# Row tiles of two GLU layers turned by DMA instead of TensorE, with 41 DMA issues moved to ScalarE's queue

## The chip, the core and the metric

The kernel runs on one core of a Trainium2 chip, in one launch. The metric is the device time of the launch in microseconds; a time without more is the median of several runs. A profiled execution, taken by the hardware profiler, has its own time, and a span: from the first recorded instruction to the last.

The engines are named as the profile names them: PE (TensorE: matmuls, and transposes, which are matmuls with the identity), PEld (its weight loads), DVE (VectorE), ACT (ScalarE), POOL (GpSimd) and SP (SyncE, which here only issues DMAs). Each runs its own instructions in order and waits on semaphores for the others. The letter q behind a name (SPq, ACTq) marks the engine's queue instructions, DMA issues among them.

## The reference: what is computed

Four residual blocks on a sequence of 2048 rows of 512 in bf16, forward, and then all gradients for a given `grad_out`. Blocks 0 and 2 are linear attention with 32 heads of 16, blocks 1 and 3 a gated linear unit (GLU) with F = 1376. Blocks 0 and 2 share their weights, and so do 1 and 3. Cut to what matters:

```python
def A(h):                                  # h = layernorm(x), no scale or shift
    q, k, v = heads(h @ wqkv)
    pq, pk = phi(q), phi(k)                # t + 1 for t > 0, else exp(t); + 1e-6
    kv, z = pk^T v, sum(pk)                # per head, over the whole sequence
    o = (pq @ kv) / (pq . z + 1e-6)
    return o @ wo

def B(h):
    g, u = h @ w_gate, h @ w_up
    return (sigmoid(g) * u) @ w_down

x = x + A(layernorm(x)); x = x + B(layernorm(x))
x = x + A(layernorm(x)); x = x + B(layernorm(x))
# returned: x, and the gradients by A_x, A_wqkv, A_wo, B_w_gate, B_w_up, B_w_down
```

## The kernel before, in words

**Layers and row tiles.** Layers are numbered 0 to 3 (0 and 2 attention, 1 and 3 GLU). The rows are cut into 16 tiles (`st`) of 128, which are handled in 8 pairs. The residual `k.xs[st]` stays on the chip. For the backward pass the forward pass stores to HBM the normalized rows (`sv_h`), of the attention the rows pq divided by their denominator (`sv_pqn`), and of the GLU the sigmoid with its derivative product (`sv_ssd`) and the gated product in 32x32 block-transposed form (`sv_hdd`, `sv_hdl`).

**The stages the change touches.** `ab_fwd` (L1058) runs twice: at L202 for layer 1, at L233 for layer 3. It does the tail of the attention layer before it (the products of turned pq rows with `kv` and `wo`, added to the residual) and the whole GLU layer. After a prelude for tiles 0 to 3 come rounds i = 1 to 7, one for each further pair, with `st = 2i` the first tile of the pair whose gate and up products are computed.

**A round.** It holds six units `gu` (L1090 and on; `CUNITS`, L1054). A unit takes two chunks of 128 columns of F for the 256 rows of the pair: eight matmuls of 256 columns into a `g` bank of PSUM, eight into a `u` bank. Unit 5 has a single chunk, so half of that. Then:

- L1106 and L1107 (ACT): sigmoid of g into `ssd_t`, sigmoid of -g into `oms`;
- L1108 (DVE): `hhT` = u times the sigmoid, which reads the `u` bank;
- L1109 (POOL): the derivative product into the second half of `ssd_t`;
- L1112 (SP): the store of `ssd_t` to `sv_ssd`.

Between the units stand, in the order written at L1186 to L1225:

- `A.attn_y` for the two tiles of the next pair (`attn_y` ends in an add on DVE to the residual, followed by the statistics of their LayerNorm);
- `A.pair_front1` and `pair_front2` (L962): for the pair two further on, DVE divides pq by its denominator (`den`, L969 and on); two DMA transposes on SP (L977) turn `pqnstage` (128x512 each) into `pqnT`; L979 stores the rows;
- `after` (L1131): in layer 1 the LayerNorm apply of the next layer, in layer 3 the rounding of the final rows into a staging tile and its store, one for each pair (`out_cb`, L221; the store is L229);
- `down_mm`: 11 matmuls of 512 columns with `w_down` for a tile of an earlier pair, and the add to the residual on DVE;
- `ln.apply(st + 2)` before unit 3 and `ln.apply(st + 3)` behind it (`FwdLN.apply`, L546): ACT writes the normalized rows (L529) into `hstage`, a pair to a buffer; the second call also issues the store to `sv_h` (L556);
- `trs`: block transposes of `hhT` on DVE (L1047, 768 columns at a time), each stored from SP (L1050, to `sv_hdd`/`sv_hdl`);
- `ln.stage_T` (L558) near the round's end: eight PE transposes (L569) of the pair's `hstage` into a bank of PSUM, and one evacuation on ACT (L380) into `hT`. `hT` is what all matmuls of the next round's units read (L1090). The rounds with a next pair, i = 1 to 6, have one;
- `fills`: turns of weight pieces for the backward pass, in small portions, and `turn_weights`: the DMAs of `fill` one by one, each ordered behind the `sv_ssd` store of the last unit. In layer 1 these are DMA transposes of weights with their stores (L429, L430), in layer 3 also 12 plain loads of turned weight pieces (L466, L468).

The units' order in rounds 1 to 6 is 0, 1, 2, 3, 5, `stage_T`, 4; in round 7, where `stage_T` does nothing, 4 and 5 follow each other (L1215, L1218).

**What sets the order.** On PE, ACT, DVE and POOL the instructions stand in the program's order. SP's order is chosen by a scheduler, so a DMA of SP need not stand where the program has it. A DMA issued from ACT (`nc.scalar.dma_start`) stands in ACT's program order, between the computing instructions. All DMAs of both queues share eight semaphores, in turn, so each waits for the one eight before it.

**Buffers.** PSUM: bank `t` x2, `g` x2, `u` x2, `y` x1, `ln` x1. SBUF: `hstage` 2 (the staging tile of the final rows in layer 3 takes turns with it), `hT` 2, `oms` 2, `ssd_t` 5 in layer 1; in layer 3 three, and two more named `ssd_q`; `pqnstage` 2, `pqnT2` 2.

Of the kernel before, what the change touches and what calls it, by code (L numbers as in the profile page):

```python
# [9 lines left out]
BF16 = mybir.dt.bfloat16  # L10
# [12 lines left out]
P = 128  # L23
NST = S // P
NDC = D // P
NFC = (F + P - 1) // P
# [39 lines left out]
def kernel(  # L66
# [18 lines left out]
    nc = tc.nc  # L85
# [3 lines left out]
    k = K()  # L89
# [4 lines left out]
    out0 = out_0.rearrange("b s d -> (b s) d")  # L94
# [52 lines left out]
    with tc.tile_pool(name="wfwd", bufs=1, reuse_waits="tile") as wfwd, ExitStack() as lctx, tc.manual_schedule(engines=EM):  # L147
# [27 lines left out]
        def load_wd():  # L175
# [16 lines left out]
            hT=lctx.enter_context(tc.tile_pool(name="ln_hT", bufs=2, reuse_waits="tile")),  # L192
# [3 lines left out]
        with tc.tile_pool(name="aq0", bufs=1, reuse_waits="tile") as aq:  # L196
            A = kq_fwd(k, aq, 0, lns[0], lns[1], x_bf)
# [5 lines left out]
        with tc.tile_pool(name="aq2", bufs=1, reuse_waits="tile") as aq:  # L203
            ocur, bw = {}, {}
            k.g_in = g_in
            k.g_from_input = 3
            k.sv[3]["gbf"] = g_in

            def open_bwd():
                xctx.close()  # L210
                bw["wb"] = bctx.enter_context(tc.tile_pool(name="wbwd", bufs=1, side="right", reuse_waits="tile"))
                prectx = ExitStack()
                k.pre = dict(pool=prectx.enter_context(tc.tile_pool(name="pre", bufs=1, side="right",
                                                                    reuse_waits="tile")), close=prectx.close)
                bw["B3"] = BBwd(k, 3)

            A = kq_fwd(k, aq, 2, lns[2], lns[3])
            open_bwd()
            wb, B3 = bw["wb"], bw["B3"]

            def out_cb(st):  # L221
                if st % 2 == 0:
                    ocur["t"] = k.lnres["stg"].tile([P, 2, D], BF16, name="out0_t", tag="hstage")
                if st >= NST - 2:
                    nc.gpsimd.tensor_scalar(ocur["t"][:, st % 2, :], k.xs[st][:], 1.0, 0.0, ALU.mult, ALU.add)
                else:
                    nc.scalar.copy(ocur["t"][:, st % 2, :], k.xs[st][:])
                if st % 2 == 1:
                    nc.sync.dma_start(out=dram_batch(out0, st // 2, 2), in_=ocur["t"][:])  # L229

            fill = Fill(wT_groups_b(k, wb), wT_dmas_b(k))
            A.tail(fill)
            ab_fwd(k, A, lns[3], fill, out_cb=out_cb, bwd=B3)  # L233

    if True:
# [80 lines left out]
        last = 2 * D // GW * NDC  # L316
# [6 lines left out]
        T = {}  # L323
# [61 lines left out]
def batch_rows(b, nb=NB):  # L385
    return slice(b * nb * P, (b + 1) * nb * P)


def dram_batch(ap2d, b, nb=NB):
    return ap2d[batch_rows(b, nb), :].rearrange("(n p) d -> p n d", p=P)  # L390
# [64 lines left out]
def wT_dmas_b(k):  # L455
    nc = k.nc
    view = lambda d: d.rearrange("(c p) f -> p c f", p=P)
    parts, h = [], F // 2
    for r0, r1, c0 in ((0, h, 0), (h, F, WDT)):
        parts.append((k.wdT[:, WDT:NDC, r0:r1], k.w_in["wd"][r0:r1, WDT * P:D],  # L460
                      [(view(k.wT["wdT"][c0 * P:(c0 + 2) * P, :]), k.wdT[:, c0:c0 + 2, :])]))
    jobs = wT_dmas(k, parts)
    for nm, t in (("wu", k.wuT), ("wg", k.wgT)):
        for c in range(0, NFC - 1, 2):
            e = c + 2
            jobs.append(lambda nm=nm, t=t, c=c, e=e: nc.sync.dma_start(out=t[:, c:e, :],  # L466
                                                                       in_=view(k.wT[nm + "T"][c * P:e * P, :])))
        jobs.append(lambda nm=nm, t=t: nc.sync.dma_start(out=view(k.wT[nm + "T"][(NFC - 1) * P:, :]),  # L468
                                                         in_=t[:, NFC - 1:, :]))
    return jobs  # L470

# [53 lines left out]
def ln_apply(k, x_t, h_out, nmr, rstd, quick=False):  # L525
    if quick:
        k.nc.vector.tensor_scalar(h_out, x_t, nmr, rstd, ALU.subtract, ALU.mult)
        return
    k.nc.scalar.activation(h_out, x_t, ACT.Identity, bias=nmr[:], scale=rstd)  # L529


class FwdLN:
# [10 lines left out]
        if st < NST:  # L543
            self.nmr[st] = ln_stats(self.k, self.k.xs[st][:], self.rstd(st), st < 1)

    def apply(self, st):  # L546
        if st >= NST:
            return
        k, nc, l = self.k, self.k.nc, self.l
        if st % 2 == 0:  # L550
            self.cur = k.lnres["stg"].tile([P, 2, D], BF16, name="hstage", tag="hstage")
        h_t = self.cur[:, st % 2, :]
        self.hs[st] = h_t
        ln_apply(k, k.xs[st][:], h_t, self.nmr.pop(st), self.rstd(st), st < 1)
        if st % 2 == 1:
            nc.sync.dma_start(out=dram_batch(k.sv[l]["h"], st // 2, 2), in_=self.cur[:])  # L556

    def stage_T(self, sts, evac="scalar", bank="ln"):  # L558
        if sts[0] >= NST:
# [341 lines left out]
def attn_fronts(k, A, pool, small):  # L901
    nc = k.nc
    sva = k.sv[A.l]
    cur, F_ = {}, {}
# [57 lines left out]
    def pair_front2(i, turned=True):  # L962
        if i >= NST // 2:
            return
        f = F_[2 * i]
        den = f["den"]
        pqn = pool.tile([P, 2, D], BF16, name="pqnstage", bufs=2)
        rden = A.rden_all[:, 2 * i:2 * i + 2, :].rearrange("p n h -> p (n h)")
        nc.vector.tensor_scalar(den[:], den[:], EPS, None, ALU.add)  # L969
        nc.vector.reciprocal(rden, den[:])  # L970
        nc.vector.tensor_tensor(pqn[:].rearrange("p n (h e) -> p (n h) e", h=H),
                                A.pq_pairs[i][:].rearrange("p n (h e) -> p (n h) e", h=H),
                                rden.unsqueeze(2).to_broadcast([P, 2 * H, DH]), ALU.mult)
        if turned:
            pqnT = pool.tile([P, 2, NDC, P], BF16, name="pqnT2", bufs=2)
            for j in range(2):
                nc.sync.dma_start_transpose(out=pqnT[:, j, :, :], in_=pqn[:, j, :])  # L977
                F_[2 * i + j] = dict(T=pqnT[:, j, :, :])
        nc.sync.dma_start(out=dram_batch(sva["pqn"], i, 2), in_=pqn[:])  # L979
        f["pqn"] = pqn  # L980

    def pair_front3(i):
        if i >= NST // 2:
# [9 lines left out]
            F_[2 * i + j] = dict(T=pqnT[:, j, :, :])  # L993

    A.pair_prod, A.pair_front1, A.pair_front2, A.pair_front3 = pair_prod, pair_front1, pair_front2, pair_front3

    def attn_mm(st, bank="y"):
        if st >= NST:
            return
        pqnT = F_[st]["T"]  # L1000
        y_ps = F_[st]["y"] = ps_tile(k, bank, [P, D], F32, "y_ps")
        for c in range(NDC):
            nc.tensor.matmul(y_ps[:], lhsT=pqnT[:, c, :], rhs=A.M_sb[:, c, :],
                             start=(c == 0), stop=(c == NDC - 1))
# [49 lines left out]
CUNITS = [(c, min(2, NFC - c)) for c in range(0, NFC, 2)]  # L1054
# [3 lines left out]
def ab_fwd(k, A, ln, fill, nxt=None, out_cb=None, bwd=None):  # L1058
    nc, tc = k.nc, k.tc
    la, l = A.l, A.l + 1  # L1060
    sva, sv = k.sv[la], k.sv[l]
    with ExitStack() as ctx:
# [114 lines left out]
        for i in range(1, NPAIR):  # L1177
            st = 2 * i
            last = i == NPAIR - 1
            nf = fill.share(i, NPAIR - 1)  # L1180

            def trs(n):
                for _ in range(min(n, len(pend))):
                    trans(*pend.pop(0))
            nt = 1 if i < NPAIR - 2 else 2
            gu(st, 2, *CUNITS[0])  # L1186
            if l == 3 and i > 1:
                turn_weights()
            A.attn_y(st + 2, "t")
            A.attn_y(st + 3, "t")  # L1190
            A.pair_front1(i + 2)
            after(st - 3)
            gu(st, 2, *CUNITS[1])
            A.pair_front2(i + 2)
            trs(nt)
            fills((nf + 2) // 3)
            gu(st, 2, *CUNITS[2])
            if l == 3 or i % 2 == 0:
                turn_weights()
            if i > 1:  # L1200
                down_mm(st - 2)
            ln.apply(st + 2)
            if last:
                trans(NBLK - 1, 0)
            gu(st, 2, *CUNITS[3])
            if l == 3:
                turn_weights()
            down_mm(st - 1, "t")
            ln.apply(st + 3)
            A.pair_prod(i + 3)  # L1210
            fills(nf // 3)
            trs(nt)
            if last:
                trans(NBLK - 1, 1)
            gu(st, 2, *CUNITS[4 if last else 5])  # L1215
            ln.stage_T([st + 2, st + 3], bank="t")
            after(st - 2)
            gu(st, 2, *CUNITS[5 if last else 4])  # L1218
            if l == 3:
                turn_weights()  # L1220
            fills((nf + 1) // 3, "vector")
            if l == 1 and last:
                nc.scalar.activation(k.tab[:], k.neg[:], ACT.Exp)
            if i % 2 == 1 and not last:
                pend += [(i // 2, g) for g in range(NG + 1)]  # L1225
            if i == NPAIR - 3 and bwd is not None:
                bwd.load_g(0)
# [920 lines left out]
```

## Time and profile before

| | |
|---|---|
| time, median of 3 runs | 1109.11 us (1108.24 to 1110.34) |
| the profiled execution's own time | 1108.52 us |
| its span | 1106.8 us |
| mean clock granted to TensorE | 0.998 of full speed |
| moved by DMA | 268.25 MB, mean 242 GB/s |
| PE transposes of `stage_T` (L569) | 128, from 69.2 to 374.3 us |
| evacuations into `hT` on ACT (L380) | 16, 1.01 us each for a pair |
| DMA transposes on SP (L977) | 20, median issue 1.26 us, from 98.2 to 354.4 us |
| stores `sv_h<-hstage` from SP | 16 of 256 KB, median 3.8 us from issue to landing |
| stores `sv_pqn<-pqnstage` from SP | 16 of 256 KB, median 2.4 us from issue to landing |

How to read it: times are microseconds from the span's start. The share of an engine is its busy time over the span, or over a window of it. A group of instructions is named by line, engine, operation and tiles, "out<-in" with shape and type. In the timeline a row has its start, its duration in us (for several instructions from the first's start to the last's end), what ran, and in brackets the idle time ahead of it with what ended it: `[0.61 <-DVE hhT L1108]` is an engine that sat idle 0.61 us until that write of DVE's, in line 1108, was done. A row of SPq with DMA_TRANSPOSE or DMA_DIRECT2D is the issuing of a DMA; the time to its landing is told apart. The two stretches of `ab_fwd`'s rounds are roughly 84 to 200 us (layer 1) and 275 to 390 us (layer 3); behind them lies the backward pass.

### The profile page before, as it was taken

Reading aid. Unit: us, or ns where it says so; the run is one execution under the profiler, and the core shown is the slowest. Engines: PE = TensorE matmul, PEld = TensorE weight load, DVE = VectorE, ACT = ScalarE, POOL = GpSimd, SP = SyncE. Lnnn points to the kernel's source line nnn. Section 1 sums busy time; section 2 is a strip of 40 time slices with the busy share of each in tenths; the row PEclk is TensorE's granted clock in tenths of the full one; section 3 lists DMA queues with packets and bytes.
Section 4 is the critical chain, followed back from the end, with each engine's and each line's share of the span. In section 5 each row is a group of like instructions: output and inputs, shape, how many; then the busy total and the mean of one; then the engine's idle time right before and its main releaser. Section 6 shows DMA issues by size and latency. Waiting matters only on the chain. (4 is left out here: it accounts for less than half of the span.)

```text
span 1106.8 us, 19893 instructions
## 1 busy us (share of the span) xinstructions
PE 1081.1 (98%) x7294; PEld 664.6 (60%) x7396; DVE 723.7 (65%) x1263; ACT 483.9 (44%) x904; POOL 462.0 (42%) x627
## 2 busy tenths in 40 slices
PE   7999999999999999999999999999999999999998
PEld 4467777546777744445666556544447855555587
DVE  7888997888888667776974630067778946632221
ACT  4767556556655524444633451235445513420001
POOL 3728676433765446774111430057881102420000
PEclk9999999999999999999999999999999999999999
DMA  7956877696698679876899978998867999958997
GB/s 216 319 181 172 224 195 236 202 265 202 191 289 223 216 236 302 298 228 229 241 262 260 260 222 286 269 327 251 242 199 224 288 253 255 264 187 282 278 253 168
DMA packets 364146, 268.25 MB, mean 242 GB/s; under 512 B 127184, under 2 KB 342672, under 8 KB 364048
## 3 DMA queue, kind: packets, MB, share of 16 engines
q1 hardware_dynamic: 364048, 266.97, 84.2%
q8 instruction: 58, 0.95, 0.4%
q14 instruction: 40, 0.33, 0.1%
HBM read 122.62 MB, written 119.47 MB: 219 GB/s over the span
## 5 line engine op out<-in xcount | busy, mean ns | idle before, releaser
L1736 PE MATMUL p_ps<-p_set,p_a 128*128 128x384 bf16 (+2 forms) x1792 | 264.1, 303 | 1.4 <-DVE dw_stg L1751 0.8
L1736 PEld LDWEIGHTS <-p_a 128*128 128x128 bf16 x1792 | 168.8, 96 | 84.7 <-DVE dw_stg L1751 1.1
L1427 POOL TENSOR_TENSOR dd<-dhb,ssd 128x512 bf16<-128x512 bf16 x84 | 96.9, 1158 | 102.1 <-ACT dhb L1425 98.7
L1426 DVE TENSOR_TENSOR dd<-dhh_ps,ssd 128x512 bf16<-128x512 f32 x85 | 57.0, 677 | 119.8 <-ACT dhb L1425 116.6
L1451 PE MATMUL dh_ps<-wuT,dd 128*128 128x512 bf16 (+1 forms) x339 | 128.5, 379 | 0.5
L1451 PE MATMUL dh_ps<-wgT,dd 128*128 128x512 bf16 (+1 forms) x329 | 124.7, 379 | 0.1
L1451 PEld LDWEIGHTS <-dd 128*128 128x128 bf16 x680 | 66.4, 98 | 79.6
L1109 POOL TENSOR_TENSOR ssd_t<-hhT,oms 128x512 bf16<-128x512 bf16 (+2 forms) x76 | 82.9, 1098 | 49.1 <-DVE hhT L1108 23.5
L1751 DVE TENSOR_TENSOR dw_stg<-p_ps,dw_stg 128x384 bf16<-128x384 f32 (+2 forms) x76 | 32.1, 438 | 105.5 <-PE p_ps L1736 100.8
L1425 ACT CAST dhb<-dhh_ps 128x512 bf16<-128x512 f32 x84 | 48.7, 589 | 114.8 <-PE dhh_ps L1419 105.7
L1090 PE MATMUL u_ps<-hT,wu 128*128 128x256 bf16 (+1 forms) x792 | 92.7, 261 | 1.2 <-DVE hhT L1108 1.1
L1090 PE MATMUL g_ps<-hT,wg 128*128 128x256 bf16 (+1 forms) x792 | 92.8, 261 | 0.6 <-ACT wt_st L380 0.3
L1047 DVE STREAM_TRANSPOSE tr_stg<-dd 128x768 f32<-128x768 f32 (+1 forms) x62 | 86.7, 1434 | 1.2
L1090 PEld LDWEIGHTS <-wg 128*128 128x128 bf16 x792 | 70.1, 98 | 17.0 <-DVE hT L378 0.9
L1419 PE MATMUL dhh_ps<-gT,wdT 128*128 128x512 bf16 x299 | 76.9, 379 | 1.9 <-DVE dd L1426 1.1
L1125 PE MATMUL y_ps<-wd,hhT 128*128 128x512 bf16 (+1 forms) x337 | 77.7, 379 | 0.8
L1090 PEld LDWEIGHTS <-wu 128*128 128x128 bf16 x792 | 70.5, 98 | 9.1 <-issue 2.1
L1106 ACT ACTIVATE ssd_t<-g_ps 128x512 bf16<-128x512 f32 (+2 forms) x76 | 42.5, 559 | 63.1 <-PE g_ps L1090 61.3
L1753 ACT CAST dw_stg<-p_ps 128x384 bf16<-128x384 f32 (+2 forms) x76 | 28.1, 386 | 83.4 <-PE p_ps L1736 81.2
L1419 PEld LDWEIGHTS <-wdT 128*128 128x128 bf16 x352 | 34.2, 98 | 42.9 <-issue 3.2
L1108 DVE TENSOR_TENSOR hhT<-u_ps,ssd_t 128x512 bf16<-128x512 f32 (+2 forms) x76 | 47.2, 629 | 17.8 <-PE u_ps L1090 11.0
L517 POOL TENSOR_TENSOR rstd_all<-rstd_all,neghalf 128x1 f32<-128x1 f32 x64 | 38.1, 595 | 47.9 <-DVE rstd_all L516 43.2
(256 smaller groups left out, 1908.3 us busy)
## 6 DMA issues: line engine op xcount, KB each, us to landing
sv_hdd<-tr_stg SPq DMA_DIRECT2D x72, 384.0 KB, 4.6
p_set<-sv_hdd SPq DMA_DIRECT2D x18, 1536.0 KB, 7.2
ssd<-sv_ssd SPq DMA_DIRECT2D x23, 768.0 KB, 5.1
sv_ssd<-ssd_t SPq DMA_DIRECT2D x61, 256.0 KB, 3.2
h_ld<-sv_h SPq DMA_DIRECT2D x30, 256.0 KB, 3.9
sv_hdl<-tr_stg SPq DMA_DIRECT2D x24, 256.0 KB, 4.7
p_a<-sv_h SPq DMA_DIRECT2D x12, 512.0 KB, 6.2
p_set<-sv_hdl SPq DMA_DIRECT2D x24, 256.0 KB, 5.2
```

Of the source, the lines that this page charges most:

```text
L1047: nc.vector.transpose(t[:, :, 0:n * P].bitcast(F32).rearrange("p q (a j) -> p q a j", a=2 * n), src.rearrange("p c x -> p (c x)").bitcast( ...
L1090: nc.tensor.matmul(ps[:, ci * n:(ci + 1) * n], lhsT=w_sb[:, kc, (c0 + ci) * P:(c0 + ci + 1) * P], rhs=hT[:, kc, (st % 2) * P:(st % 2) * P ...
L1106: nc.scalar.activation(ssd[:, :, 0, :], gv, ACT.Sigmoid)
L1108: nc.vector.tensor_tensor(hh, uv, ssd[:, :, 0, :], ALU.mult)
L1109: nc.gpsimd.tensor_tensor(ssd[:, :, 1, :], hh, oms, ALU.mult)
L1125: nc.tensor.matmul(y_ps[:], lhsT=h[0:r, fc, off:off + P], rhs=k.wd[0:r, fc, :], start=(fc == 0), stop=(fc == NFC - 1))
L1419: nc.tensor.matmul(ps[:], lhsT=k.wdT[:, jc, u * P:(u + 1) * P], rhs=self.gT[B][:, jc, :], start=(jc == 0), stop=(jc == NDC - 1))
L1425: nc.scalar.copy(dhb[:], ps[:])
L1426: nc.vector.tensor_tensor(self.dd[ng][:, 0, c, :], ps[:], self.ssd[ng][:, c, 0, :], ALU.mult)
L1427: nc.gpsimd.tensor_tensor(self.dd[ng][:, 1, c, :], dhb[:], self.ssd[ng][:, c, 1, :], ALU.mult)
L1451: nc.tensor.matmul(self.acc[j][:], lhsT=dd[0:r, a, c, j * P:(j + 1) * P], rhs=w[0:r, u, :], start=(u == 0 and a == 0), stop=(u == NFC - 1 ...
L1736: nc.tensor.matmul(ps[:, 0:w], lhsT=lhs[:, s, ic * P:(ic + 1) * P], rhs=rhs, start=(s == 0), stop=(s == NST - 1))
```

## The change

1. `FwdLN.apply` gets an argument `turned`. With it, the apply of each row tile is followed by a DMA transpose on SP from `hstage` into `hT`, and the `sv_h` store is issued by ACT.
2. In `ab_fwd`'s rounds both applies stand together ahead of unit 3, `turned`. `stage_T` is gone from the rounds (the prelude keeps its own), and unit 4 comes before unit 5 in every round.
3. The `sv_pqn` store of the rounds moves out of `pair_front2` into `pair_store`, behind unit 3, and is issued by ACT.
4. The stores of the final rows (but for the last pair) and the 12 plain loads of weight pieces in layer 3 are issued by ACT.

In the order of instructions there are 96 PE transposes and 12 evacuations on ACT fewer, 24 DMA transposes more on SP, and 41 DMAs that go from SP to ACT (12 `sv_h` stores, 10 `sv_pqn` stores, 7 stores of final rows, 12 weight pieces). The number of instructions on DVE and POOL does not change.

```diff
@@ -226,7 +226,7 @@
                 else:
                     nc.scalar.copy(ocur["t"][:, st % 2, :], k.xs[st][:])
                 if st % 2 == 1:
-                    nc.sync.dma_start(out=dram_batch(out0, st // 2, 2), in_=ocur["t"][:])
+                    (nc.sync if st >= NST - 2 else nc.scalar).dma_start(out=dram_batch(out0, st // 2, 2), in_=ocur["t"][:])
 
             fill = Fill(wT_groups_b(k, wb), wT_dmas_b(k))
             A.tail(fill)
@@ -463,9 +463,9 @@
     for nm, t in (("wu", k.wuT), ("wg", k.wgT)):
         for c in range(0, NFC - 1, 2):
             e = c + 2
-            jobs.append(lambda nm=nm, t=t, c=c, e=e: nc.sync.dma_start(out=t[:, c:e, :],
-                                                                       in_=view(k.wT[nm + "T"][c * P:e * P, :])))
-        jobs.append(lambda nm=nm, t=t: nc.sync.dma_start(out=view(k.wT[nm + "T"][(NFC - 1) * P:, :]),
+            jobs.append(lambda nm=nm, t=t, c=c, e=e: nc.scalar.dma_start(out=t[:, c:e, :],
+                                                                         in_=view(k.wT[nm + "T"][c * P:e * P, :])))
+        jobs.append(lambda nm=nm, t=t: nc.scalar.dma_start(out=view(k.wT[nm + "T"][(NFC - 1) * P:, :]),
                                                          in_=t[:, NFC - 1:, :]))
     return jobs
 
@@ -543,17 +543,21 @@
         if st < NST:
             self.nmr[st] = ln_stats(self.k, self.k.xs[st][:], self.rstd(st), st < 1)
 
-    def apply(self, st):
+    def apply(self, st, turned=False):
         if st >= NST:
             return
         k, nc, l = self.k, self.k.nc, self.l
         if st % 2 == 0:
+            if turned:
+                self.hTs[st // 2] = k.lnres["hT"].tile([P, NDC, 2, P], BF16, name="hT")
             self.cur = k.lnres["stg"].tile([P, 2, D], BF16, name="hstage", tag="hstage")
         h_t = self.cur[:, st % 2, :]
         self.hs[st] = h_t
         ln_apply(k, k.xs[st][:], h_t, self.nmr.pop(st), self.rstd(st), st < 1)
+        if turned:
+            nc.sync.dma_start_transpose(out=self.hTs[st // 2][:, :, st % 2, :], in_=h_t)
         if st % 2 == 1:
-            nc.sync.dma_start(out=dram_batch(k.sv[l]["h"], st // 2, 2), in_=self.cur[:])
+            (nc.scalar if turned else nc.sync).dma_start(out=dram_batch(k.sv[l]["h"], st // 2, 2), in_=self.cur[:])
 
     def stage_T(self, sts, evac="scalar", bank="ln"):
         if sts[0] >= NST:
@@ -976,8 +980,14 @@
             for j in range(2):
                 nc.sync.dma_start_transpose(out=pqnT[:, j, :, :], in_=pqn[:, j, :])
                 F_[2 * i + j] = dict(T=pqnT[:, j, :, :])
-        nc.sync.dma_start(out=dram_batch(sva["pqn"], i, 2), in_=pqn[:])
+            cur["rows"] = pqn
+        else:
+            nc.sync.dma_start(out=dram_batch(sva["pqn"], i, 2), in_=pqn[:])
         f["pqn"] = pqn
+
+    def pair_store(i):
+        if i < NST // 2:
+            nc.scalar.dma_start(out=dram_batch(sva["pqn"], i, 2), in_=cur["rows"][:])
 
     def pair_front3(i):
         if i >= NST // 2:
@@ -993,6 +1003,7 @@
             F_[2 * i + j] = dict(T=pqnT[:, j, :, :])
 
     A.pair_prod, A.pair_front1, A.pair_front2, A.pair_front3 = pair_prod, pair_front1, pair_front2, pair_front3
+    A.pair_store = pair_store
 
     def attn_mm(st, bank="y"):
         if st >= NST:
@@ -1199,23 +1210,23 @@
                 turn_weights()
             if i > 1:
                 down_mm(st - 2)
-            ln.apply(st + 2)
+            ln.apply(st + 2, True)
+            ln.apply(st + 3, True)
             if last:
                 trans(NBLK - 1, 0)
             gu(st, 2, *CUNITS[3])
+            A.pair_store(i + 2)
             if l == 3:
                 turn_weights()
             down_mm(st - 1, "t")
-            ln.apply(st + 3)
             A.pair_prod(i + 3)
             fills(nf // 3)
             trs(nt)
             if last:
                 trans(NBLK - 1, 1)
-            gu(st, 2, *CUNITS[4 if last else 5])
-            ln.stage_T([st + 2, st + 3], bank="t")
+            gu(st, 2, *CUNITS[4])
             after(st - 2)
-            gu(st, 2, *CUNITS[5 if last else 4])
+            gu(st, 2, *CUNITS[5])
             if l == 3:
                 turn_weights()
             fills((nf + 1) // 3, "vector")
```

## The prediction

> **What bounds the kernel now.** First the page: span, busy shares and slices.
>
> ```profile
> span 1106.8 us, 19893 instructions
> PE 1081.1 (98%) x7294; PEld 664.6 (60%) x7396; DVE 723.7 (65%) x1263; ACT 483.9 (44%) x904; POOL 462.0 (42%) x627
> ```
>
> TensorE is the bound on the average. The change touches two stretches alone, the pair rounds of layers 1 and 3 (`ab_fwd`), so I read their windows (one round of layer 1, one of layer 3; columns: us, busy of PE, PEld, DVE, ACT, POOL, clock, DMA share, GB/s).
>
> ```profile
> 117.00:134.00 17.00, 16.81 (x130) 12.18 (x130) 15.96 (x25) 9.76 (x18) 12.47 (x19) 1.00 0.94 238
> 307.00:324.00 17.00, 16.89 (x131) 12.39 (x131) 14.51 (x21) 9.42 (x17) 11.06 (x14) 1.00 1.14 279
> ```
>
> PE is full in both, but in layer 1 DVE has 1 us free of 17, and in layer 3 the DMA engines have nothing free. Then the timeline at the seam of two rounds (layer 1, round 6 to 7; first PE, then DVE):
>
> ```profile
> 183.42 0.61 PE L569 MATMUL ln_tp<-ident,hstage 128*128 128x128 bf16 x8
> 183.87 1.04 PE L1090 MATMUL g_ps<-hT,wg 128*128 128x256 bf16 x8
> 184.74 1.04 PE L1090 MATMUL u_ps<-hT,wu 128*128 128x256 bf16 x8
> 185.61 1.04 PE L1090 MATMUL g_ps<-hT,wg 128*128 128x256 bf16 x8
> 187.26 1.03 PE L1090 MATMUL u_ps<-hT,wu 128*128 128x256 bf16 x8 [0.61 <-DVE hhT L1108]
> ```
> ```profile
> 184.37 2.53 DVE L1047 STREAM_TRANSPOSE tr_stg<-hhT 128x768 f32<-128x768 f32 x2
> 186.82 0.98 DVE L1108 TENSOR_TENSOR hhT<-u_ps,ssd_t 128x256 bf16<-128x256 f32 x2
> ```
>
> There are two `u` banks, so the first unit of a round (unit 0) waits at its `u` matmuls until DVE has read the unit two before it. Now that is the small unit 5 (256 columns, 0.38 us on DVE), since unit 4 comes last. The start of unit 0's `u` in rounds 3, 4, 6 and 7 of layer 1 lags what PE alone would give by 0.25, 0.19, 0.32 and 0.77 us, each ending 0.05 us after that read; into round 5 there is no lag.
>
> **What is removed.** `stage_T` of 12 pairs (6 in each layer): 96 turns on PE. From start to start (183.42 to 183.87, less one 0.055 us step) eight of them hold PE 0.447 us, the same in all 12 places: 12 x 0.447 = **5.4 us** of a full engine, the whole of what can be won. A round of PE alone falls from 16.53 to 16.09 us. The 12 evacuations on ACT (L380, 1.01 us each) go too; ACT is busy 9.8 of 17 us, so that wins nothing by itself.
>
> The Trainium skill speaks against this trade ("VectorE: DVE Perf Modes", "Rules for kernel authors"): turn 128x128 on TensorE if a PSUM destination is acceptable, by DMA otherwise. Its section "The three transpose paths" has 390 ns for TensorE, by which the 96 turns would be worth 37 us (an estimate); the trace has 56 ns each, and it decides.
>
> **Unit 4 and unit 5 change places.** Without `stage_T` the order is 4, 5, then unit 0. Unit 0 now waits for DVE's read of unit 4 (0.68 us) in place of that of unit 5 (0.38), both directly behind the block transposes on DVE. In layer 1 DVE runs back to back from the attention add of a round to the end of this read (timeline 121.77 to 136.5, no gap over 0.04), so PE coming 0.45 earlier doesn't help: the loop is DVE's work, 0.05, `u` of unit 0 (1.04), 0.1, and again. It gets 0.30 longer at the ends of rounds 2, 3, 5 and 6, and 0.06 at round 4, where unit 4 was late: +1.26. Round 1 has no block transposes and keeps its gain: -0.45. In layer 3 the two LayerNorm statistics of the next layer are missing on DVE (2 x 0.87 us); there unit 4's read would end at 309.8, and PE, 0.45 earlier, wants it at 310.4: hidden by 0.5 us.
>
> **The new DMA turns on SP.** 24 issues. The nearest row is the same shape, `pqnT<-pqnstage` (L977): 1.26 us of SP each in layer 1, landing 2.4 to 2.6 us after the issue; in layer 3:
>
> ```profile
> 305.13 3.10 SPq L977 DMA_TRANSPOSE pqnT<-pqnstage  x2
> 320.06 2.92 SPq L977 DMA_TRANSPOSE pqnT<-pqnstage  x2
> 336.59 3.94 SPq L977 DMA_TRANSPOSE pqnT<-pqnstage  x2
> ```
>
> where landing takes 3.2 to 4.8. The packets of one (512 of 256 B at 20 ns over 16 engines) are 0.64 us of all DMA engines, 1.3 us a round: little, except at a share of 1.14. What counts is where they stand on SP, which the order of the changed instructions shows; unit 0 needs both of a pair.
> - Layer 1, rounds 1 to 5: both stand before the `pqnT` turns, behind LayerNorm's apply. Round 4: second issue about 161.7, landed about 164.3, wanted at 168.3. Hidden; `pqnT` lands about 168 for 171.
> - Layer 1, round 6: behind unit 2's `ssd` store, L430 and the weight turn L429 (181.48 to 183.16). Issues at 183.2 and 184.5, landed 187.1 to 187.8; DVE lets unit 0 begin at 186.7. +0.4 to +1.1, taken **+0.6**.
> - Layer 3, rounds 1 and 5: both early, gain kept. Round 6: behind unit 2's store (370.94), landed 375.2, wanted 375.6: hidden by 0.4, gain kept. 3 x -0.447 = **-1.3**.
> - Layer 3, rounds 2 to 4: the first turn stands before the two `pqnT`, the second behind them, the `sv_hdd` store and unit 2's `ssd` store, which itself waits for POOL. Round 2:
>
> ```profile
> 301.22 1.16 POOL L1109 TENSOR_TENSOR ssd_t<-hhT,oms 128x512 bf16<-128x512 bf16 x1 [0.51 <-DVE den L969]
> 305.64 2.35 POOL L1109 TENSOR_TENSOR ssd_t<-hhT,oms 128x512 bf16<-128x512 bf16 x2 [3.26 <-ACT hstage L529]
> ```
>
> Unit 1's store goes at 302.4; the first apply ends about 303.0 (ACT's oms ends 301.5, a weight piece now stands before it, 0.7, apply 0.81); first turn 303.05 to 304.3; two `pqnT` 2.5 to 3.9; `sv_hdd` and `ssd` store 0.65 and 0.7 with their gaps: second turn issued 308.2 to 309.6, landed (2.4 to 4.8) at 310.6 to 314.4. Even with SP free, POOL's product (306.8) and the store before it put the landing at 309.8 or later. PE wants it at 309.5 (309.95 - 0.45). **PE stops 1.1 to 4.9 us**. I take 2.0, near the low end, because the `pqn`, `h`, `out` stores and two or three weight pieces (3 to 4 us of SP a round) leave this queue, and a longer round thins the DMA load: net 2.0 - 0.45 = +1.55, three times: **+4.7** (bounds +2.0 and +13.4).
>
> **The stores and pieces on ACT's queue.** 41 issues. No row shows one there; SP's rows for them are 0.36 to 0.84 us (one at 1.26), so I take 0.55, 22.5 us in all, against the 12 us of evacuations gone. Each stands in ACT's program order. The `h` store follows the second apply and holds the sigmoid of unit 3, the `pqn` store that of unit 4; ACT idles 2.34 and 1.9 us just there (`[2.34 <-PE g_ps L1090]`, `[1.91 <-PE g_ps L1090]`), and DVE wants unit 3's sigmoid over 1.5 us later still. In layer 3 the pieces before unit 0 and unit 1 hold sigmoids that DVE reads 0.8 to 3 us after they are made. Cost 0 while an issue stays under about 1 us. Its lower bound isn't below nothing: ACT ends no wait of PE in these rounds. Upper bound: rival C.
>
> **Sum** on the profiled execution (1108.52 us; span 1106.8 and 1.7 around it): -0.45 + 1.26 + 0.6 - 1.3 + 4.7 = **+4.8**, so 1113.3. The execution lies 0.6 below the median shown (1109.11); against that: **1113.9**.
>
> **Rivals.**
> - *A, not slower: the second turn lands in time* (place: SP in layer 3, rounds 2 to 4; decides at an issue up to 307.1, that is 309.5 less 2.4). Then layer 3 gives 6 x -0.447 = -2.7, layer 1 stays at +1.4: -1.3, **1107.8**. For it: SP is relieved, and with the weight pieces on another queue turns may land at layer 1's 2.5. Against: POOL's product alone ends at 306.8.
> - *B, all is hidden*: DVE also keeps pace in layer 1. -5.4, **1103.7**. Against: the four lags above already end at DVE's read, and its work there is untouched.
> - *C, ACT becomes late*: an issue on ACT lasts as long as a turn running on SP, 0.55 + 1.26 to 2.67; the `h` store falls into the four turns by construction. Beyond 2 us unit 3's sigmoid, then DVE, are late: up to 1 us in 10 rounds, or the DMA backlog lands the turns at the upper bound: +9 to +16, **1121**.
> - That the change does not do what it says is excluded: the instruction order has 24 more DMA turns on SP, 41 DMAs on ACT, 96 turns fewer on PE.
>
> For C the Trainium skill has a mechanism ("Perfetto Trace Analysis", DMA Instruction, HWDGE): the descriptor generator is shared by the two issuing sequencers and locked, and the wait for the lock is inside the profiled issue. No run here has two queues issuing.
>
> **How the numbers follow.** Forecast 0.52 (1110.9 to 1118), A 0.18 (1106.5 to 1109), B 0.13, C 0.17 (1118 to 1125). The range leaves out B and half of C: **1106.5 to 1121**. A measurement of this kernel tells about 0.2% (2.2 us) from no change. Faster than that: B and the edge of A, 0.16; within: A and the forecast's low edge, 0.19; slower: 0.65.
>
> **What would show it.** Right: L569 is gone from the rounds; PE at unit 0's `g` in layer 3, rounds 2 to 4, waits 1 to 3 us for a DMA into `hT`; unit 0's `u` in layer 1 waits 0.5 to 1 us for DVE's 512-column read; rounds of 17.0 to 17.1 us there; layer 3's round 5 at 16.09. Wrong: rounds of 16.1 us in layer 1 (the DVE loop fails); in layer 3 the second turn issued before 307 (the SP chain fails); ACT issues over 1 us, or PE or DVE waiting for ACT (C).

## The result, and the profile after

The changed kernel takes **1134.76 us** (median of 4 runs, 1132.91 to 1138.45) against 1109.72 us for the kernel before in the same comparison: ratio 1.023, 95% interval 1.021 to 1.0249. It is slower, as forecast, but by 25 us where the forecast had 4.8 and its range ended at 1121. The profiled execution is the slowest of the four (1138.45 us, span 1136.7), so its trace holds some 3.7 us more than the median.

The page of the changed kernel, its span, busy shares, and the group of the gate matmuls (columns: busy us, mean ns, idle time ahead of them with its main cause):

```profile
span 1136.7 us, 19761 instructions
PE 1083.5 (95%) x7198; PEld 661.1 (58%) x7300; DVE 724.8 (64%) x1263; ACT 471.6 (41%) x892; POOL 461.5 (41%) x627
...
L1101 PE MATMUL g_ps<-hT,wg 128*128 128x256 bf16 (+1 forms) x792 | 95.8, 266 | 23.9 <-DMA hT<-hstage 14.1
```

L1101 is L1090 of before. These matmuls waited 0.6 us in all before, now 23.9, most of it for the DMA turns. PE's share falls from 98% to 95%: it has no more work, it waits. The waits of PE between 85 and 400 us (total, times, longest):

```profile
PE g_ps L1101 <- DMA hT<-hstage: 13.7, 4, 8.2
PE g_ps L1101 <- issue: 8.2, 2, 5.5
PE u_ps L1101 <- DVE hhT L1119: 1.7, 3, 0.7
```

The waits put down to "issue" are of the same kind: in both, the second hT turn lands 0.09 us before the matmul starts.

Where in the forward pass? From the timeline of PE I took the start of unit 0's first matmul in every round. The table has the time from one to the next, in us; round 7 goes to the start of its last unit.

| rounds | 1 | 2 | 3 | 4 | 5 | 6 | 7 |
|---|---|---|---|---|---|---|---|
| layer 1, before | 14.68 | 16.54 | 16.79 | 16.72 | 16.54 | 16.85 | 14.26 |
| layer 1, changed | 15.59 | 16.09 | 16.98 | 17.67 | 17.95 | 18.85 | 15.15 |
| layer 3, before | 14.31 | 16.54 | 16.54 | 16.54 | 16.54 | 16.54 | 13.49 |
| layer 3, changed | 14.37 | 24.47 | 23.86 | 20.95 | 17.76 | 16.68 | 13.49 |

The sums are +5.9 us in layer 1 and +21.1 in layer 3, 27.0 of the 29.9 us between the two spans. Of the rest, 0.5 was won ahead of layer 1's first unit, and 3.4 stand behind layer 3. There nothing changed, and the same stretch took 717.2 to 721.2 us over all traces of this study, in no order of the kernels (717.2 before, 721.2 in e9, which is as fast as before), so I don't count it as an effect. How far one trace can be trusted here: e4, e5, e6 and e10 below have the changed kernel's order of instructions in the rounds of layer 1, on SP too, and these rounds add up to 116.2, 116.5, 119.9 and 116.2 us, against 118.3 here and 112.4 before. So a difference of up to 4 us between two single traces need not come from an edit.

The heart of it is the end of round 2 of layer 3. PE first, then SP:

```profile
323.38 1.86 PE L1101 MATMUL g_ps<-hT,wg 128*128 128x256 bf16 x8 [8.22 <-DMA hT<-hstage]
325.04 1.91 PE L1101 MATMUL u_ps<-hT,wu 128*128 128x256 bf16 x8
327.18 1.91 PE L1014 MATMUL y_ps<-M_sb,pqnT 128*128 128x512 bf16 x7 [0.22 <-issue]
328.92 1.04 PE L1101 MATMUL g_ps<-hT,wg 128*128 128x256 bf16 x8
```
```profile
310.19 2.30 SPq L558 DMA_TRANSPOSE hT<-hstage  x1
312.58 3.48 SPq L981 DMA_TRANSPOSE pqnT<-pqnstage  x2
316.15 0.55 SPq L1061 DMA_DIRECT2D sv_hdd<-tr_stg  x1
316.80 0.58 SPq L1123 DMA_DIRECT2D sv_ssd<-ssd_t  x1
317.47 1.76 SPq L558 DMA_TRANSPOSE hT<-hstage  x1
```

The order on SP is the one the prediction read: one turn, the two pqnT turns, `sv_hdd`, unit 2's store, and only then the second turn. It lands at 323.29, 5.8 us after its issue began, and PE, which had been ready at 315.2, starts 0.09 us later. Rounds 3 and 4 have the same order: the first turn is issued 11.5 us into the round, the two pqnT turns and the two stores follow without a gap, and the second turn comes at 17.2 and 17.1 us. And see the first three rows of PE: eight matmuls take 1.86 us, where the same eight take 1.04 five microseconds later. The clock shows why (window, PE, PEld, DVE, ACT, POOL, granted clock, DMA share, GB/s):

```profile
316.00:320.00 4.00, 0.00 (x0) 0.00 (x0) 1.12 (x2) 2.15 (x5) 1.90 (x3) 0.68 0.95 265
320.00:324.00 4.00, 0.62 (x4) 0.45 (x5) 0.00 (x0) 0.00 (x0) 0.00 (x0) 0.50 1.21 245
324.00:328.00 4.00, 3.78 (x17) 2.40 (x17) 0.69 (x1) 1.59 (x3) 0.11 (x1) 0.54 0.59 181
328.00:332.00 4.00, 4.00 (x35) 3.15 (x33) 3.60 (x7) 1.34 (x3) 2.51 (x6) 1.00 0.39 126
```

While PE waits, its clock falls to half, and it stays there for the first matmuls after the wait. Unit 0 to unit 1 takes 5.54 us in place of 3.47. So this wait costs 2.1 us more than it lasts.

### The profile page after: what moved, and what is told of

It reads as the page before. It is cut to its first block, busy times and chain, and to the rows that moved or that the text cites. A ratio compares the mean times of both kernels' runs of the same rounds, so it can differ in the third digit from the quotient of the medians.

```text
span 1136.7 us, 19761 instructions
## 1 busy us (share of the span) xinstructions
PE 1083.5 (95%) x7198; PEld 661.1 (58%) x7300; DVE 724.8 (64%) x1263; ACT 471.6 (41%) x892; POOL 461.5 (41%) x627
## 5 line engine op out<-in xcount | busy, mean ns | idle before, releaser
L1101 PE MATMUL g_ps<-hT,wg 128*128 128x256 bf16 (+1 forms) x792 | 95.8, 266 | 23.9 <-DMA hT<-hstage 14.1
L1120 POOL TENSOR_TENSOR ssd_t<-hhT,oms 128x512 bf16<-128x512 bf16 (+1 forms) x76 | 83.3, 1103 | 73.1 <-DVE hhT L1119 35.5
L1101 PE MATMUL u_ps<-hT,wu 128*128 128x256 bf16 (+1 forms) x792 | 96.2, 267 | 1.7 <-DVE hhT L1119 1.7
L1101 PEld LDWEIGHTS <-wg 128*128 128x128 bf16 x792 | 71.1, 99 | 43.9 <-issue 23.4
L1117 ACT ACTIVATE ssd_t<-g_ps 128x512 bf16<-128x512 f32 (+1 forms) x76 | 42.8, 563 | 98.1 <-PE g_ps L1101 81.1
L1101 PEld LDWEIGHTS <-wu 128*128 128x128 bf16 x792 | 72.2, 100 | 10.8 <-issue 2.2
L1119 DVE TENSOR_TENSOR hhT<-u_ps,ssd_t 128x512 bf16<-128x512 f32 (+1 forms) x76 | 47.5, 633 | 42.6 <-PE u_ps L1101 35.6
L1118 ACT ACTIVATE oms<-g_ps 128x512 bf16<-128x512 f32 (+1 forms) x96 | 53.8, 560 | 9.7 <-POOL ssd_t L1120 9.7
```

Source lines behind the costliest of these rows:

```text
L1101: nc.tensor.matmul(ps[:, ci * n:(ci + 1) * n], lhsT=w_sb[:, kc, (c0 + ci) * P:(c0 + ci + 1) * P], rhs=hT[:, kc, (st % 2) * P:(st % 2) * P ...
L1118: nc.scalar.activation(oms, gv, ACT.Sigmoid, scale=-1.0)
L1119: nc.vector.tensor_tensor(hh, uv, ssd[:, :, 0, :], ALU.mult)
L1120: nc.gpsimd.tensor_tensor(ssd[:, :, 1, :], hh, oms, ALU.mult)
```

## The experiments

Two theories after the result. **Theory 2, the place:** the second turn stands too far back on SP and lands too late. **Theory 1, ACT:** a DMA that ACT issues waits, in ACT's program order, for the landing of the DMA eight before it; applies and sigmoids are late, and the turns with them. ACT's timeline in the changed kernel shows that this happens:

```profile
301.79 0.61 ACT L227 CAST out_t<-x 128x512 bf16<-128x512 f32 x1
305.29 0.41 ACTq L229 DMA_DIRECT2D out_dram<-out_t  x1
305.81 0.60 ACT L1117 ACTIVATE ssd_t<-g_ps 128x512 bf16<-128x512 f32 x1 [3.41 <-DMA wdT_d<-wdT]
```

The store's issue takes 0.41 us, but ACT, done with its cast at 302.40, could only issue it when a weight store that SP had issued at 299.61 had landed, at 305.22; both signal the same semaphore.

### e1: the turns without ACT's queue

```diff
 # e1, against the changed kernel; likewise the pqn and final rows' stores and the weight pieces
-            (nc.scalar if turned else nc.sync).dma_start(out=dram_batch(k.sv[l]["h"], st // 2, 2), in_=self.cur[:])
+            nc.sync.dma_start(out=dram_batch(k.sv[l]["h"], st // 2, 2), in_=self.cur[:])
```

> The DMA turns and the order 4, 5 of the changed kernel, but all 41 stores and pieces issued by SP again. Theory 1 (ACT's DMA issues: each waits in ACT's program order for the landing of the DMA eight before it, which is a slow one of SP's; so ACT's sigmoids and applies are late, and the turns with them): most of the 25 us goes, 1109 to 1117 us, and PE's wait for hT stays under 3 us in each round. Theory 2 (the turns themselves: their place on SP and 4 to 6 us to landing): 1122 to 1135 us, with waits of 5 to 8 us left in layer 3.

1121.4 us, ratio 1.009 (1.0065 to 1.0116): between the two. Layer 1 loses 1.7 us in place of 5.9. In layer 3 rounds 4 to 6 take 16.09 us each, the turn's 0.45 us fully won, but round 2 takes 24.14 and round 3 18.67. SP in round 2 of this kernel, where the first apply had ended at 305.92:

```profile
306.42 0.70 SPq L466 DMA_DIRECT2D wuT<-wuT_d  x1
307.21 0.53 SPq L229 DMA_DIRECT2D out_dram<-out_t  x1
307.84 0.43 SPq L1123 DMA_DIRECT2D sv_ssd<-ssd_t  x1
308.37 3.14 SPq L981 DMA_TRANSPOSE pqnT<-pqnstage  x2
...
314.44 2.82 SPq L558 DMA_TRANSPOSE hT<-hstage  x2
```

Between the end of the apply and the turns stand the two pqnT turns and seven other DMAs. Theory 1 can't make this wait (7.89 us at PE), since ACT issues no DMA here.

### e2: ACT's queue without the turns

```diff
 # e2, against the kernel before; likewise the pqn (behind unit 3) and final rows' stores and the weight pieces
-            nc.sync.dma_start(out=dram_batch(k.sv[l]["h"], st // 2, 2), in_=self.cur[:])
+            (nc.scalar if act else nc.sync).dma_start(out=dram_batch(k.sv[l]["h"], st // 2, 2), in_=self.cur[:])
```

> The kernel before (turns on PE, order 5, turn, 4) with the 41 DMAs issued by ACT. Theory 1: slower than before by 6 to 18 us, with ACT waiting 2 to 3 us at a time for DMAs in layer 3, and PE for ACT's or DVE's results. Theory 2: within 2 us of before (1108 to 1112).

1111.45 us, ratio 1.0004 (0.9991 to 1.0018): no difference that can be told. ACT's waits are there:

```profile
ACT ssd_t L1113 <- DMA sv_ssd<-ssd_t: 2.8, 1, 2.8
ACT hstage L529 <- DMA sv_ssd<-ssd_q: 2.5, 1, 2.5
```

In the trace only round 2 of layer 3 is longer (19.48, +2.9 us), where PE waits for ACT's apply and evacuation; all other rounds are as before.

```profile
PE g_ps L1097 <- ACT hT L380: 1.7, 1, 1.7
PE ln_tp L569 <- ACT hstage L529: 0.9, 1, 0.9
```

So ACT's queue can make PE wait without any DMA turn; over several executions, the interval leaves it at most 2.0 us.

### e3 and e7: the units' order

```diff
 # e3, against the kernel before
-            gu(st, 2, *CUNITS[4 if last else 5])
+            gu(st, 2, *CUNITS[4])
             ln.stage_T([st + 2, st + 3], bank="t")
             after(st - 2)
-            gu(st, 2, *CUNITS[5 if last else 4])
+            gu(st, 2, *CUNITS[5])
```

> The kernel before with units 4 and 5 in the order 4, turn, 5, turns on PE. The step of the prediction that prices this (unit 0 waits for DVE's read of unit 4 in layer 1): +0.3 us a round in layer 1, 1110 to 1111 us, and u of unit 0 lags by 0.5 us or more. If DVE keeps pace: within 0.3 us of before.

e3: 1113.46 us, ratio 1.003 (1.0017 to 1.0044). But nearly every round, of layer 3 too, takes 16.92 us, and PE waits 12 times for ACT's evacuation into `hT`, which the small unit 5 alone now covers. That is a cost of e3, not of the change, so the question went to e7:

```diff
 # e7, against the kernel before (ln.apply(st + 3) also goes up, to ln.apply(st + 2))
-            gu(st, 2, *CUNITS[4 if last else 5])
             ln.stage_T([st + 2, st + 3], bank="t")
+            gu(st, 2, *CUNITS[4])
             after(st - 2)
-            gu(st, 2, *CUNITS[5 if last else 4])
+            gu(st, 2, *CUNITS[5])
```

> The kernel before, all turns on PE and all DMAs on SP, with both applies ahead of unit 3, the PE turn ahead of unit 4, and then units 4 and 5. It isolates the step on the units' order: the turn's evacuation is covered by two units, and unit 0 waits for DVE's read of unit 4. By the prediction rounds 2 to 6 of layer 1 take about 0.25 us longer (16.8 to 17.1), layer 3 stays at 16.54: 1111 to 1112 us. If DVE has room: layer 1 as before, within 0.5 us of before.

e7: 1112.55 us, ratio 1.0015 (1.0003 to 1.0027). Layer 1's rounds 3 to 7 are 0.34, 0.13, 0.06, 0.38 and 0.28 us longer than before, 1.18 with round 1's -0.01; layer 3's rounds 1 to 6 are as before, round 7 0.05 longer. The seam of rounds 6 and 7, as the prediction showed it for before:

```profile
186.19 1.04 PE L1090 MATMUL g_ps<-hT,wg 128*128 128x256 bf16 x8
188.12 1.03 PE L1090 MATMUL u_ps<-hT,wu 128*128 128x256 bf16 x8 [0.89 <-DVE hhT L1108]
```

The lag of unit 0's `u` behind DVE grows from 0.61 to 0.89 us, by the 0.3 us that DVE's read of unit 4 takes more.

### e4, e5, e6: the place and ACT's queue, two by two

```diff
 # e4: the changed kernel, final rows' stores and weight pieces on SP again
 # e5: the changed kernel, pqnT behind both hT turns
+  with tc.issue_after(ln.turn):      # the second hT turn
+      A.pair_turn(i + 2)             # the two pqnT turns, taken out of pair_front2
 # e6: e4, with the second hT turn of rounds 2 to 4 of layer 3 behind unit 2's store
+  with self.k.tc.issue_after(behind):
+      nc.sync.dma_start_transpose(out=self.hTs[st // 2][:, :, st % 2, :], in_=h_t)
```

> The changed kernel with the final rows' stores and the weight pieces (19 DMAs, all in layer 3) on SP again; the h and pqn stores stay on ACT. Layer 1 as in the changed kernel. Theory 1: most of layer 3's 21 us goes, 1113 to 1121 us. Theory 2: layer 3 stays as it is or gets worse by the longer queue on SP, 1132 to 1140 us.

> The changed kernel, all 41 DMAs still on ACT, with one thing moved: on SP the two pqnT turns of a round are put behind both hT turns (in layer 3, rounds 2 to 4, they stood between them). If the place of the second hT turn on SP is the cost: its issue comes at 12.5 to 14 us into the round in place of 17.1 to 18.6, rounds 2 to 4 of layer 3 take 16.5 to 18.5 us in place of 24.5, 23.9 and 21.0, and the time is 1117 to 1125 us. If ACT's waits ahead of its DMA issues are the cost (late applies): no more than 5 us are won, 1129 to 1135.

> The counterpart: the kernel e4 (final rows and weight pieces on SP), in which both hT turns stood ahead of pqnT, with the second hT turn of rounds 2 to 4 of layer 3 put behind the pqnT turns and unit 2's ssd store, as it stands in the changed kernel. If the place is the cost: 3 to 6 us more in each of the three rounds than e4's 17.75, 17.2 and 16.5, the TensorE clock falling in the wait, 1127 to 1135 us. If ACT's waits are: within 3 us of e4 (1117.6).

With only these stores and pieces moved, e4 takes 1117.6 us, but on SP its two turns also came to stand together, ahead of pqnT. So e4 changed both suspects at once; e5 (1122.16 us) and e6 (1136.15 us) part them. Ratio to before, and in brackets the rounds 1 to 7 of layer 3 in sum (110.5 before):

| | final rows and pieces on ACT | on SP |
|---|---|---|
| second turn behind pqnT and the stores | changed: 1.023 (131.6) | e6: 1.0223, 1.0202 to 1.0244 (129.9) |
| both turns ahead of pqnT | e5: 1.0105, 1.0076 to 1.0134 (116.1) | e4: 1.0057, 1.0038 to 1.0075 (112.1) |

The place is worth 15.5 and 17.8 us of layer 3, far more than the 4 us by which two traces differ without cause. ACT's queue comes out at 1.7 and 4.0, which is not clear of that; the ratios of the first row can't be told apart, and in the second e4 and e5 also differ in the order of the pqnT turns and stores behind the hT turns. e6's time is 1 us above what was expected; 3.7 us of its trace over e4's stand in layer 1, which the edit doesn't touch. e6 brings the long wait back with the 19 DMAs on SP:

```profile
324.12 1.87 PE L1105 MATMUL g_ps<-hT,wg 128*128 128x256 bf16 x8 [7.07 <-DMA hT<-hstage]
```

Theory 2 holds; Theory 1 is at most a second, smaller cost. Nor does e5 come out free: in round 3 (21.19 us, expected up to 18.5) PE now waits for the pqnT turns that were put back, and the clock falls in that wait.

```profile
PE y_ps L1018 <- DMA pqnT<-pqnstage: 3.5, 2, 3.3
PE g_ps L1105 <- DMA hT<-hstage: 1.9, 2, 1.6
```

### e8 and e11: can the queue be mended?

```diff
 # e8: e4 with the turns on ACT, right behind their applies
-  nc.sync.dma_start_transpose(out=self.hTs...
+  nc.scalar.dma_start_transpose(out=self.hTs...
 # e11: e1 with pqnT and its store behind both hT turns (as in e5)
```

> The kernel e4 with the 24 hT turns issued by ACT, each right behind its apply, so that nothing of SP's queue stands ahead of them. If the place on SP is what is left of e4's loss: layer 1's rounds 5 and 6 fall from 18.3 and 18.8 to below 17, layer 3's rounds to 16.1 to 16.6, and the time to 1108 to 1113 us. If issuing a turn on ACT (1.2 us or more each, ahead of unit 3's sigmoid) makes DVE late: 1115 to 1125 us.

> The kernel e1 (DMA turns in all 12 rounds, all stores on SP) with the pqnT turns and the sv_pqn store of each round put behind both hT turns on SP. Theory of the place: round 2 of layer 3 falls from 24.1 to 17 to 18.5 us, round 3 from 18.7 to 16.5 or so with the clock kept, and the time to 1111 to 1115 us; a smaller wait comes up at pqnT. If round 2's wait has another cause than the place: 1119 or more.

e8: 1121.85 us (1.0094, 1.0074 to 1.0114); the second case came. PE hardly waits for `hT` any more, but for ACT, which issues the turns between its sigmoids, and for DVE, which in turn waited 21.8 us for ACT's `ssd_t` (4.9 in e4):

```profile
PE u_ps L1101 <- DVE hhT L1119: 8.7, 11, 2.0
PE g_ps L1101 <- ACT oms L1118: 4.0, 6, 1.0
PE y_ps L1014 <- DMA pqnT<-pqnstage: 2.6, 2, 1.4
PE g_ps L1101 <- DMA hT<-hstage: 0.4, 1, 0.4
```

The third row has a cause of its own. In all ten rounds with pqnT turns SP issued the first of them only 0.13 to 0.16 us after ACT's second hT turn had landed, so the turns of the two queues followed each other.

e11: 1123.67 us (1.0111, 1.0098 to 1.0125), no better than e1: my expectation of 1111 to 1115 was wrong. The wait for `hT` went, and a larger one came at pqnT:

```profile
PE y_ps L1018 <- DMA pqnT<-pqnstage: 12.0, 6, 4.4
PE g_ps L1105 <- DMA hT<-hstage: 1.8, 1, 1.8
```

I had taken the place for a matter of order alone. Where SP also has the stores and pieces, as in e1 and e11, it is one of room too: four turns a round, issued in 1.2 to 2 us each, on a queue that already issued for 13.8 and 14.4 of the 16.5 us of rounds 2 and 3 before. There whichever turn is last tends to make PE wait; that this is a matter of room is argued, not tested by itself. Room doesn't explain rounds 3 and 4 of the changed kernel: SP issued for 10.6 of 23.9 and 9.1 of 20.9 us there, and e5, by order alone, takes 16.09 us in round 4.

### e9: only the rounds that win

```diff
 # the kernel before, with DMA turns (and 4, 5) in five of the twelve rounds
+  turned = (l, i) in ((1, 1), (3, 1), (3, 4), (3, 5), (3, 6))
```

> The kernel before, all stores on SP, with DMA turns (and the order 4, 5) in five of the twelve rounds alone: round 1 of layer 1 and rounds 1, 4, 5, 6 of layer 3, those that took 0.45 us less in e1. Theory of the place: both turns of these rounds land before they are wanted, each round wins 0.45 us, 2.2 us in all, about 0.998 of before (0.997 to 0.999). Rival (the turns disturb by being there, whatever their place): same as before or slower, 1.000 to 1.005.

1109.61 us, ratio 0.9992 (0.9983 to 1.0001): not to be told from before, and between the two expectations, so it decides for neither. The forward rounds are 1.2 us shorter in its trace, about half of what was expected: rounds 1 of both layers and round 5 of layer 3 win their 0.45 us, rounds 4 and 6 only 0.10, and round 3, turned on PE, loses 0.68 (PE waits 0.73 us there for a pqnT turn). The rest is spread over rounds that were not turned.

### e10: the clock

```diff
+  for _ in range({3: 34, 4: 22, 5: 9}[i]):       # ahead of unit 0, layer 3
+      nc.tensor.matmul(idle_ps[:], lhsT=k.ident[:], rhs=k.wd[:, 0, :], start=True, stop=True)
```

> The changed kernel with PE kept busy in its three long waits: 34, 22 and 9 matmuls of 512 columns more, into an unused bank, ahead of unit 0 in rounds 3, 4 and 5 of layer 3 (their result is not used). If the falling clock is a cost of its own: granted clock 1.00 in these rounds, unit 0 to unit 1 in 3.5 us again in place of 5.6, 5.6 and 5.1, and 4 to 6 us less than the changed kernel (1128 to 1131). If the slow matmuls after a wait come from something else (DMA load): no gain, 1134 or more.

In the profiled execution (1130.5 us) the clock holds at 1.00 in all of layer 3, and unit 0 to unit 1 of rounds 3 to 5 takes 3.47 us again:

```profile
313.07 7.50 PE L1200 MATMUL idle_ps<-wd,ident 128*128 128x512 bf16 x33
321.25 1.03 PE L1101 MATMUL g_ps<-hT,wg 128*128 128x256 bf16 x8 [0.68 <-issue]
```

Layer 3's rounds add up to 125.8 us, 5.8 less than in the changed kernel. So in this trace the slow matmuls do come from the idle time. The time does not confirm the size; by it alone the second case came: 1134.95 us in the median (ratio 1.0241, 1.0209 to 1.0273), between 1130.5 and 1142.9. The profiled execution is the fastest of the four, that of the changed kernel the slowest of its four, and the other three of e10 show a clock of 0.994 to 0.997 again. How much of the 25 us the clock holds in the median stays open.

### e12: why layer 1 lost more than in e1

```diff
 # e4, sv_h and sv_pqn stores behind unit 5
   gu(st, 2, *CUNITS[5])
+  ln.store(st + 3)
+  A.pair_store(i + 2)
```

> The kernel e4 with the sv_h and sv_pqn stores, still issued by ACT, moved from between the applies and unit 4 to behind unit 5, so that their packets no longer run beside the hT turns. It asks why layer 1 lost 5.9 us in the changed kernel and only 1.7 in e1, where SP issued these stores. If they slow the turns' landing (4.1 us for the second turn of round 1, 3.3 in e1): round 1 of layer 1 falls from 15.6 to 14.3 to 14.6 us, layer 1 by 2 to 4 us, and the time to 1113 to 1116 us. If the place on SP alone sets the landing: round 1 stays at 15.4 to 15.6, and the time within 2 us of e4 (1117.6).

1117.8 us, as e4. Round 1 of layer 1 did fall, from 15.57 to 14.39 us: the second turn is issued 10.75 us into the round in place of 11.36 and lands 3.5 us later in place of 4.1 (e1: 3.3). So the two ACT stores beside the turns cost that round its 1.2 us, half in the issue and half in the landing. But round 6 rose to 20.24 (PE waits 3.1 us for the turn there), layer 1 as a whole won 1.2 us and not 2 to 4, which two traces can differ by without cause, and the time did not move. What layer 1 lost beyond that in the changed kernel is in part the clock (1.7 us in round 7); the rest stays open.

## Why the prediction was wrong, step by step

By the table the forecast's +4.8 us stands against +27.0: layer 1 +5.9 in place of +1.4, rounds 1, 5 and 6 of layer 3 +1.4 in place of -1.3, rounds 2 to 4 of layer 3 +19.7 in place of +4.7. The sign was right; the last of these terms holds 15.0 of the 22.2 us that were missed.

- **The removed turns, 0.447 us a pair: right.** Wherever both DMA turns were in time, a round of PE alone took 16.09 us (round 2 of layer 1 in the changed kernel, rounds 4 to 6 of layer 3 in e1).
- **Units 4 and 5 change places, +1.26 with 0.45 us off for round 1: right.** e7 has +1.18 for the exchange in its trace, and 1.7 us (0.3 to 3.0) by its ratio; round 1's gain is in e1 and e9 (14.23 us against 14.68).
- **Layer 1, rounds 1 to 5, "hidden": wrong.** Rounds 1, 4 and 5 lost 0.9, 0.95 and 1.4 us. The second issue of round 5 (the prediction calls it round 4) was put at 9.5 us into the round; it came at 13.5, since the applies ended at 10.5 and 11.2 and the first turn took 2.2 us. Landings took 3.4 to 5.2 us in these rounds, where I used pqnT's 2.4 to 2.6. e1 has 2.4 to 4.3; e12 shows ACT's stores as part of the difference in round 1.
- **Layer 1, round 6, +0.6: the mechanism right.** Second issue 16.2 us into the round, where 15.7 was expected, landed at 18.7, within the 18.3 to 19.0 expected. What was missing is the clock: after this wait round 7 took 15.15 us, against 13.49 in e1 and e4.
- **Layer 3, rounds 1, 5 and 6, -1.3: wrong, +1.4.** Rounds 1 and 6 end 0.5 and 0.6 us later than PE alone would, 0.09 and 0.14 us after the second turn's landing; round 5 is in time but pays 1.7 us of slow clock for the wait before it.
- **Layer 3, rounds 2 to 4, +4.7: the failed step.** Order and mechanism were as written, the size was not: +7.9, +7.3 and +4.4. PE's wait was taken as 2.0 us, bounds 1.1 to 4.9; it measured 8.2, 5.5 and 2.6, which is 16.4 of the 19.7. In round 2 the chain came apart link by link: the first apply ended 11.25 us into the round, not 9.6 (ACT's 2.8 us of waiting ahead of the `out` store); the first turn's issue took 2.3 us, not 1.25; so the second issue came at 18.55, not at 14.8 to 16.2; and it landed 5.8 us later, beyond the 4.8 of the range. I took the low end because SP was to be relieved. In round 2 it was not: SP issued for 20.0 of its 24.5 us. In rounds 3 and 4 it was (10.6 and 9.1 us), and it didn't help: the second turn still stood behind the first, the two pqnT turns and two stores, came at 17.2 and 17.1 us and landed 6.6 and 3.7 us later. e6 and e5 show that this place is the cause; why the landings took up to 6.6 us stays open.
- **The clock, not in the sum at all.** Half speed at the start of rounds 3, 4 and 5 of layer 3: 2.07, 2.08 and 1.67 us, 5.8 in the profiled execution, and 1.66 in round 7 of layer 1. My bounds for a wait ended at the wait.
- **ACT's queue at nothing "while an issue stays under 1 us": true of the issue, 0.37 us each, and beside the point.** The issue is short; the wait ahead of it, for a landing on a shared semaphore, is not (2.8 us in round 2). The kernel's description names these semaphores, the sum gave them no price. What ACT's queue costs by itself is not settled: the traces have layer 3 longer by 2.9 us without the turns (e2) and by 1.7 and 4.0 with them, and e2's time does not show it (ratio 1.0004).
- **The rivals.** A fell with the second turn's place, B with that and with e7. C came nearest with 1121. Its first way, ACT's issues lasting as long as a turn, did not come; its second, turns landing at the upper bound, came in round 2 of layer 3 and went beyond the bound, but the second turn's place on SP decided it.

Two rules of the Trainium skill bear on this. "TensorE: Matmul & The Clock Gate", Part 1, of the Trainium skill says that the array's clock halves after an idle window of about 3.4 us, in windows that run free of the kernel. The trace agrees on the windows: by its clock record the four stretches at half clock in the changed kernel's rounds start at 191.1, 317.4, 344.7 and 368.6 us and last 3.4, 10.2, 6.8 and 3.4 us, and these times are whole multiples of 3.413 us apart. It does not agree on the length. In e8 the clock fell to half in a wait of 1.98 us, and in e12 a wait of 3.07 us left it full, as the first matmuls behind each show (first e8, then e12):

```profile
193.38 1.87 PE L1101 MATMUL u_ps<-hT,wu 128*128 128x256 bf16 x8 [1.98 <-DVE hhT L1119]
```
```profile
188.58 1.03 PE L1106 MATMUL g_ps<-hT,wg 128*128 128x256 bf16 x8 [3.07 <-DMA hT<-hstage]
```

So in these traces the length of a wait of 2 to 3 us does not decide whether it costs the clock. Its place in the windows may; no run tests that.

The Trainium skill, "DMA: Bandwidth & Descriptors", section "Issuing engines are not separate DMA queues", says that another issuing engine saves only the time of the issue, as all run on the same engines; that the turn lands after 3.5 us in e12, where ACT's stores come later, and after 4.1 in e4 agrees.

## What to carry to other kernels

A transfer that replaces work in program order is only as early as its place on its queue: write out that queue for a full round, with the measured issue times, and see what stands between its source and it, and whether the round has room for it, before pricing any stall. A store on a computing engine's queue may wait there for another queue's landing; it is free only where what stands behind it has that time to give. And when the bound engine is made to wait for microseconds, add the slow clock after the wait to its price.

## What the runs showed of the hardware that I had not expected

- The issue of a DMA turn is not a constant: 1.19 to 2.30 us for the same 128x512 turn in the changed kernel (median 1.48), median 1.22 in e1, where SP issues the stores, and in e12, where ACT issues them behind unit 5. Landing took 2.5 to 6.6 us (median 4.2), against a median of 2.7 in e1.
- Where a wait of PE brought the half clock in the changed kernel, it lasted until 3.8 to 4.4 us after the first matmul (eight of 256 columns in 1.86 us in place of 1.04), which put 1.7 to 2.1 us on top of the wait.
- The clock can fall when the wait is already over: in layer 1 PE starts again at 190.17 us, and the clock is 1.00 from 187 to 191 us and 0.57 from 191 to 195.
